# First DFT of the filters: from 64-row tiles with a zero-padded table to tiles of 32 rows and 64 columns

## The chip, the cores and the metric

The kernel runs on one core of a Trainium2 chip. The metric is the time of one execution in microseconds on the device. Five engines work side by side, each with its own list of instructions: TensorE (PE in the profile; its weight loads are listed apart as PEld), VectorE (DVE), ScalarE (ACT), GpSimd (POOL) and SyncE (SP, which here issues most of the DMA transfers). They wait for each other through semaphores.

## The reference

The block takes a sequence of 2048 positions and 512 channels through two parts, each behind a layer norm modulated by six vectors from a conditioning vector. The first part is a long convolution: for each channel a filter K of 2048 taps is built from complex exponentials, and the input is convolved with it by FFTs of length 4096. The second mixes neighbouring positions and channels with four weight matrices.

```python
P = jnp.exp(logdA[:, :, None] * l[None, None, :])
K = jnp.einsum("dn,dnl,dn->dl", Cc, P, dB).real
...
Kf = rfft2(Kp); Uf = rfft2(up)          # K and u padded to twice their length
y = irfft2(Uf * Kf)[..., :L]
y = y.transpose(0, 2, 1) + u * Dskip
...
x = x + ga * A(h)                       # the convolution
x = x + gb * B(h)                       # the MLP part
```

## The kernel before

All stages run from one program whose order is written out by hand (`tc.manual_schedule()`): each engine executes its instructions in the order of the Python calls, and the waits follow from the tiles that they read and write.

1. Filters. `turns`, `exps`, `products` and `burst` (L498) build the filters of all channels and leave them in the SBUF tile KX, 128 partitions by 8192 floats: 64 groups g of 128 floats. Beside that, the input is normalized and goes through its own first DFT (`u_dft`, L426); the result is written to the DRAM tensor VU.
2. `k_first` (L619 to L634), the stage that is changed: the filters' first DFT. The four blocks of 32 partitions of KX each hold 32 points of a different part of the filters, and each needs the same DFT of 32 points by 64 outputs. The groups' floats are the weights (the stationary side); the table FK is the moving side. Eight rounds r of eight groups; each round fills four PSUM banks: one from the pool tile pk1, one from pz, and two named pk2 (through `kbank`). pk1 and pz have two buffers each, pk2 has four, so two rounds fit. ScalarE copies two of the banks into VK[0], VectorE the other two into VK[1] (L632).
3. Sixteen steps over (jh, kc). `spectrum_u` (L650) does the input's second DFT for one block of VU, in two banks named pk1; ScalarE copies them to `us`. `spectrum_k` (L680) does the filters' second DFT from VK[jh] and the twiddle table T2, in two banks pk2. `multiply` (L690, L692) takes the products on VectorE, `back` (L702) transforms on TensorE, ScalarE copies into `z` (two buffers), and GpSimd stores z to the DRAM tensors ZT (L706). SyncE loads the blocks of VU in advance (`load_vu`, L640, seven buffers) and also x (L724), whose tile X2 is the memory of KX.
4. `inverse` (L731) loads ZT back (L721), does the last DFT and adds to x; then comes the second part with its weight matrices (lines L803 to L962), which fills the rest of the time, from some 310 us on.

The order around the change is fixed by the calls: `load_vu` of step 0, `flip(0)` on GpSimd, a small table, the eight rounds of `k_first` with the loads of the next two blocks between them, `spectrum_u` of step 0, and then for each step `spectrum_k`, `multiply`, `back` of the step before and `spectrum_u` of the step after.

Before, FK has two rows of 32 in each half of the partitions and two halves of 64 columns, with zeros where row block and column half do not belong together: one matmul over 64 partitions thus does two blocks, and its 128 columns hold the two results side by side. A bank holds four groups of one 64-row half.

Of the kernel before, what the change touches and what calls it, by code (L numbers as in the profile page):

```python
# [7 lines left out]
F32 = mybir.dt.float32  # L8
# [19 lines left out]
def shape_constants():  # L28
    f = lambda x: np.ascontiguousarray(x.astype(np.float32))
    k1, k2, q = np.arange(32), np.arange(64), np.arange(32)  # L30
    c2b = lambda c: np.where(c < 32, 31 - c, c)
    th = 2 * np.pi * (k1[None] + .5) * q[:, None] / 64
    W = np.stack([np.cos(th), -np.sin(th)], 1)
    Wt = W.transpose(0, 2, 1)
    FU = np.stack([np.stack([Wt, -Wt[..., ::-1]], 1), np.stack([Wt, Wt[..., ::-1]], 1)])
    FU = np.stack([FU, FU])
    FK = np.zeros((2, 2, 32, 2, 64))
    FK[:, 0, :, 0] = FK[:, 1, :, 1] = W.reshape(32, 64)
    b = c2b(np.arange(64))
    al = 2 * np.pi * b[:, None, None] * ((k1[None, :, None] + .5) / 4096 + k2[None, None, :] / 64)  # L40
    c, s = np.cos(al), np.sin(al)
    T2 = np.stack([np.stack([c, -s], 2), np.stack([s, c], 2)]).reshape(128, 32 * 128)
    be = np.arange(32) + .5
    al = 2 * np.pi * be[:, None, None] * ((k1[None, :, None] + .5) / 4096 + k2[None, None, :] / 64)
    TU = np.stack([np.cos(al), np.sin(al), np.cos(al), -np.sin(al)]).reshape(128, 32 * 64)
    al = 2 * np.pi * be[None, :] * k2[:, None] / 64
    cs = np.stack([np.cos(al), np.sin(al)], 2).reshape(64, 64)
    Gm = np.tile(np.concatenate([cs, cs], 1), (2, 1))
    sg = np.array([1.0, -1.0])[:, None]
    th = 2 * np.pi * (k1[:, None, None, None] + .5) * (sg * be[:, None, None] + 64 * q) / 4096  # L50
    FI = np.stack([np.cos(th), -sg * np.sin(th), -np.sin(th), -sg * np.cos(th)]) * (2 / 4096)
    eye = np.eye(16)
    j = np.arange(32)
    c0 = np.tile((eye[:, :, None] * (j + .5)).reshape(16, 512), (2, 1))
    C0 = np.zeros((2, 2, 32, 2, 512))
    C0[:, 0, :, 0], C0[:, 1, :, 1] = c0, c0
    C0 = C0.reshape(128, 1024)
    e1 = (eye[:, :, None] * j).reshape(16, 512)
    e2 = (eye[:, :, None] * np.ones(32)).reshape(16, 512)
    C1 = np.concatenate([e1, e1, e2, e2] * 2, 0)  # L60
    ex0 = np.concatenate([np.arange(31, -1, -1), np.arange(32, 64)])
    ex1 = np.concatenate([64 * np.arange(8), 512 * np.arange(4)])
    CE = np.concatenate([(eye[:, :, None] * ex0.reshape(2, 32)[:, None, None, :]).transpose(1, 0, 2, 3).reshape(16, -1),
                         np.zeros((16, 64 * NX1))], 1)
    CE = np.tile(CE, (8, 1))
    for u in range(4):
        CE[u * 32:u * 32 + 32, 1024 + u * 16 * NX1:1024 + (u + 1) * 16 * NX1] = \
            np.tile((eye[:, :, None] * ex1).reshape(16, -1), (2, 1))
    PA = np.zeros((2, 4, 16, 2, 2, 4, 2, 16))
    PB = np.zeros((4, 2, 16, 4, 4, 2, 4, 16))  # L70
    for e in range(16):
        for v in range(2):
            for u in range(4):
                for p in range(2):
                    PA[v, u, e, v, p, u, p, e] = 1
        for c in range(8):
            for p in range(4):
                PB[c // 2, c % 2, e, c // 4 * 2 + c % 2, p, 1 - c // 2 % 2, p, e] = 1
    return {k: f(v) for k, v in dict(
        FU=FU.reshape(128, 128), FK=FK.reshape(128, 128), T2=T2, TU=TU, G=Gm,  # L80
        FI=FI.reshape(128, 32 * 64), C0=C0, C1=C1, CE=CE, PA=PA.reshape(128, 512), PB=PB.reshape(128, 2048), ID=np.eye(128)).items()}


# [23 lines left out]
def body(ctx, tc, A):  # L107
    nc = tc.nc
    V, S, P, T, Y = nc.vector, nc.scalar, nc.gpsimd, nc.tensor, nc.sync
# [4 lines left out]
    def act(out, in_, f=AF.Copy, scale=1.0, bias=0.0):  # L114
        return S.activation(out, in_, f, bias=bias, scale=scale)  # L115
# [54 lines left out]
    pa12 = a12.enter_context(pool("a12"))  # L170
# [2 lines left out]
    X2 = KX.rearrange("p (b d) -> p b d", b=16)  # L173
    up = a12.enter_context(pool("up", bufs=2))
    wml = a12.enter_context(pool("wml"))
    FK = pa12.tile([128, 128], F32, name="FK")
    sp1 = pa12.tile([128, 1], F32, name="sp1")
    V.memset(sp1, 0.0)
    for i in range(4):
# [4 lines left out]
    ph = a1.enter_context(pool("ph"))  # L184
    FU = ph.tile([128, 2, 64], F32, name="FU")
    DS = ph.tile([128, 128], F32, name="DS")
# [93 lines left out]
    with tc.manual_schedule():  # L280
# [6 lines left out]
        for k, t in (("PA", PA.rearrange("p a b c -> p (a b c)")), ("CE", CE), ("C0", C0),  # L287
                     ("PB", PB.rearrange("p a b c -> p (a b c)")), ("C1", C1)):
            P.dma_start(t, A[k])
        Y.dma_start(FU, A["FU"].rearrange("p (a b) -> p a b", a=2))  # L290
        P.memset(cst, MAGIC)
# [7 lines left out]
        P.tensor_copy(ON.rearrange("p a b -> p (a b)"), cst[:, :384])  # L299
        Y.dma_start(FK, A["FK"])  # L300
        V.tensor_scalar(ld[:, 4:], cT, -1.0, None, op0=OP.mult)
# [118 lines left out]
    def u_dft(b, eo):  # L420
        x = ut[b // 4]
        ps = [psu.tile([128, 512], F32, name="pu") for h in range(2)]
        for i in range(2):
            for h in range(2):
                j = slice(64 * h, 64 * h + 64)
                T.matmul(ps[h][i * 64:i * 64 + 64], FU[j, eo], x[j, b % 4 + i],  # L426
                         start=True, stop=True, skip_group_check=True)
# [79 lines left out]
    for k in range(8):  # L507
        w, i = ("w3", k) if k < 4 else ("w4", k - 4)
        n = A[w].shape[0] // 4
# [18 lines left out]
    T2, TU = [], []  # L528
# [18 lines left out]
    with tc.manual_schedule():  # L547
# [49 lines left out]
        for f in later:  # L597
# [8 lines left out]
    TU = TU[0]  # L606
    Gm = c2.tile([128, 2, 64], F32, name="Gm")
    FI = c2.tile([128, 32, 2, 32], F32, name="FI")
    VK = [v0x.enter_context(pool("v0", side="right")).tile([128, 64, 2, 64], F32, name="VK0"),
          c2.tile([128, 64, 2, 64], F32, name="VK1")]  # L610
# [3 lines left out]
    psa = s2x.enter_context(pool("psa", bufs=2, space=PSUM))  # L614
    psb = s2x.enter_context(pool("psb", bufs=4, space=PSUM))
    kbank = lambda shape: psb.tile(shape, F32, name="pk2")
    block = lambda: ldp.tile([128, 4, 256], F32, name="ld")

    def k_first(r):  # L619
        bank = lambda n: psa.tile([128, 4, 2, 64], F32, name=n)  # L620
        ps = [bank("pk1"), kbank([128, 4, 2, 64]), bank("pz"), kbank([128, 4, 2, 64])]
        kv = KX.rearrange("p (g x) -> p g x", g=64)
        for gl in range(8):
            for j in range(2):
                rows = slice(64 * j, 64 * j + 64)
                T.matmul(ps[2 * j + gl // 4][:, gl % 4].rearrange("p j x -> p (j x)"), kv[rows, r * 8 + gl], FK[rows],  # L626
                         start=True, stop=True)
        for q in (0, 2, 1, 3):
            g0 = r * 8 + q % 2 * 4
            o, i = VK[q // 2][:, :, :, g0:g0 + 4], ps[q].rearrange("p g j x -> p x j g")  # L630
            if q // 2:
                V.tensor_copy(o, i)  # L632
            else:
                act(o, i)  # L634
# [29 lines left out]
    def spectrum_k(jh, kc):  # L664
        p = [kbank([128, 2, 2, 128]) for gh in range(2)]
        for i in range(2):
            for ro in range(2):
                for ri in range(2):
                    for kk in range(2):
                        for gh in range(2):  # L670
                            k1 = kc * 4 + 2 * kk + i
                            rows = slice(gh * 64, gh * 64 + 64)
                            w = T2[k1 // 16][rows, k1 % 16]
                            if ri == gh:
                                w = w[:, ro * 64:ro * 64 + 64]
                            elif ro == ri:
                                w = w[:, gh * 64:gh * 64 + 64]
                            else:
                                w = t3s[kc // 2 * 2][rows, k1 % 8]
                            T.matmul(p[gh][kk * 64:kk * 64 + 64, i, ro], w,  # L680
                                     VK[jh][rows, ri * 32 + k1].rearrange("p j g -> p (j g)"),
                                     start=(ri == 0), stop=(ri == 1), skip_group_check=True)
        return p
# [114 lines left out]
    def transposed(x):  # L798
        ps = [psT.tile([128, 2, 256], F32, name=f"pT{j}") for j in range(2)]
        for j in range(2):  # L800
            for i in range(2):
                for k in range(2 * j, 2 * j + 2):
                    T.transpose(ps[j][:, k % 2, i * 128:i * 128 + 128], x[:, i, k * 128:k * 128 + 128], ident)  # L803
        return ps
# [292 lines left out]
    with tc.manual_schedule():  # L1097
# [3 lines left out]
        for r in range(8):  # L1101
            k_first(r)
            if r == 3:
                load_vu(*steps[1])
            if r == 6:
                load_vu(*steps[2])
        us = spectrum_u(*steps[0])
        split = None
        for n, st in enumerate(steps):
            p = spectrum_k(*st)  # L1110
# [145 lines left out]
        n = cm.tile([128, 2, 512], F32, name="h2")  # L1256
# [18 lines left out]
        r = transposed(n)  # L1275
        split_w(1)
        r = parts_of(r)
# [4 lines left out]
        for g in range(8):  # L1282
            r = chan(g, r)
# [18 lines left out]
```

## Time and profile before

| | |
|---|---|
| runs | 687.0, 689.6, 690.3 us; median 689.6 us |
| the profiled execution | 691.26 us, of which its span (first to last instruction) 689.5 us |
| TensorE | busy 642.6 us, 93% of the span |
| VectorE | busy 498.0 us, 72% |
| ScalarE | busy 331.2 us, 48% |
| GpSimd | busy 124.8 us, 18% |
| granted TensorE clock, mean | 0.989 |
| DMA moved | 86.42 MB, mean 125 GB/s |
| `k_first` on TensorE | from 209.3 to 224.5 us |

How to read the rows that follow. In the profile, L626 is line 626 of the kernel. A row of a group names line, engine and operation, the tiles as out<-in with buffer numbers left out (pk stands for pk1 and pk2), the tile of the array as rows\*columns, the shape, and how many. A float32 matmul appears as two records, each a weight load and a matmul. In the timeline the first number is the start in us from the start of the span, the second the length; brackets give the idle time before and what ended it. In the chain that ended last, each row is a piece of the path, with start, length and place. The rows of the DMA queues give packets, MB and the share of 16 engines' time.

### The profile page before, as it was taken

How to read it: one execution, taken by the hardware profiler on the slowest of the kernel's cores; microseconds unless marked ns; L12 is line 12 of the kernel's file. 1: busy time of each engine (PE TensorE's matmuls, PEld its weight loads, DVE VectorE, ACT ScalarE, POOL GpSimd, SP SyncE). 2: the span in 40 equal slices, each digit the busy share in tenths (PEclk: the TensorE clock that was granted, in tenths of full speed). 3: DMA queues.
4: the chain of work that ended last, by engine and by line, in shares of the span. 5: the costliest groups of instructions: out<-in, count | busy, mean ns of one | idle time of the engine just before them, and what ended most of it. 6: DMA issues, size and time to landing. Idle time of an engine off the chain costs nothing.

```text
span 689.5 us, 16884 instructions
## 1 busy us (share of the span) xinstructions
PE 642.6 (93%) x7195; PEld 509.2 (74%) x7195; DVE 498.0 (72%) x795; ACT 331.2 (48%) x505; POOL 124.8 (18%) x236
## 2 busy tenths in 40 slices
PE   1899999999999998977998999999999999999996
PEld 0456655655569776634887889999899889898895
DVE  7899999999996887986987967464574536363522
ACT  3878988889875557432444623123131312222121
POOL 4011112112103355413741101001010000000000
PEclk9999999999999999998999999999999999999999
DMA  8603264643739997967387010020100201010001
GB/s 299 284 2 79 75 218 105 209 121 85 275 85 317 354 335 258 346 204 226 108 257 240 1 32 32 16 77 15 47 31 17 77 1 62 1 49 13 1 31 31
DMA packets 51091, 86.42 MB, mean 125 GB/s; under 512 B 4676, under 2 KB 39496, under 8 KB 48424
## 3 DMA queue, kind: packets, MB, share of 16 engines
q1 hardware_dynamic: 46712, 66.74, 30.1%
q0 software_dynamic: 3440, 17.57, 7.4%
q8 instruction: 56, 0.92, 0.6%
q10 hardware_dynamic: 864, 1.05, 0.5%
q14 instruction: 19, 0.16, 0.1%
HBM read 59.12 MB, written 32.90 MB: 133 GB/s over the span
## 4 chain that ended last, share of the span: by engine, by line
PE 70%; DVE 6%; DMA 5%; ACT 3%; POOL 2%; issue 1%; ACTq 0%; SPq 0%; DVEq 0%; POOLq 0%
PE pm L841 7%; PE pm L838 7%; PE pm L839 7%; PE xx L448 7%; PE pa L954 6%; PE pa L955 6%; PE pa L962 6%; PE kp L498 3%; DMA ZT<-z 3%; PE ph L893 2%; PE ph L895 2%; PE ph L892 2%; DMA ld<-ZT 2%; PE pu L426 2%; PE pT L803 2%; PE pk L626 2%
## 5 line engine op out<-in xcount | busy, mean ns | idle before, releaser
L115 ACT ACTIVATE gh<-pm 128x512 fp32r<-128x512 f32 (+1 forms) x48 | 26.9, 560 | 200.7 <-PE pm L841 200.7
L838 PE MATMUL pm<-nh,w3h 128*128 128x256 f32 (+1 forms) x352 | 86.6, 281 | 2.7 <-ACT nh L115 2.7
L839 PE MATMUL pm<-nh,w3l 128*128 128x256 f32 (+1 forms) x352 | 86.3, 280 | 0.1
L946 DVE TENSOR_TENSOR gl<-gf,gh 128x512 fp32r<-128x512 f32 (+1 forms) x48 | 30.8, 643 | 68.4 <-ACT gf L115 68.4
L954 PE MATMUL pa<-w4h,gh 128*128 128x512 f32 (+1 forms) x176 | 69.6, 395 | 0.0
L838 PEld LDWEIGHTS pm<-nh,w3h 128*128 128x128 f32 (+1 forms) x352 | 66.0, 187 | 4.4 <-ACT nh L115 2.9
L955 PE MATMUL pa<-w4l,gh 128*128 128x512 f32 (+1 forms) x176 | 68.9, 392 | 0.0
L839 PEld LDWEIGHTS pm<-nh,w3l 128*128 128x128 f32 (+1 forms) x352 | 65.9, 187 | 2.2 <-DVE w3l L756 0.5
L765 POOL TENSOR_TENSOR rs<-mv,eps_t 128x1 f32<-128x1 f32 (+1 forms) x39 | 11.0, 282 | 282.4 <-DVE mv L771 265.4
L841 PE MATMUL pm<-nl,w3h 128*128 128x256 f32 (+1 forms) x352 | 55.0, 278 | 0.0
L449 PE MATMUL xx<-MG,ON 64*128 64x512 f32 x160 | 48.1, 397 | 0.0
L962 PE MATMUL pa<-w4h,gl 128*128 128x512 f32 (+1 forms) x176 | 48.0, 390 | 0.0
L448 PE MATMUL xx<-MG,ON 64*128 64x512 f32 x160 | 48.0, 396 | 0.0
L841 PEld LDWEIGHTS pm<-nl,w3h 128*128 128x128 f32 (+1 forms) x352 | 47.0, 187 | 0.0
L898 DVE TENSOR_TENSOR h<-h,ph 128x512 f32<-128x512 f32 x16 | 11.0, 687 | 45.1 <-PE ph L895 45.1
L466 DVE SCALAR_TENSOR_TENSOR e<-tr,p 128x512 f32<-128x512 f32 x64 | 41.1, 684 | 1.5 <-ACT tr L115 1.5
L498 PEld LDWEIGHTS kp<-e,e 128*32 128x32 f32 x2048 | 30.1, 110 | 12.7 <-issue 7.6
L475 DVE TENSOR_TENSOR e<-tr,p 128x1024 f32<-128x1024 f32 x32 | 39.0, 1220 | 0.0
L476 DVE TENSOR_TENSOR e<-tr,m 128x1024 f32<-128x1024 f32 x32 | 39.0, 1219 | 0.0
L115 ACT ACTIVATE p<-xx 128x1024 f32<-128x1024 f32 (+1 forms) x40 | 37.5, 979 | 2.2 <-PE xx L252 1.0
L962 PEld LDWEIGHTS pa<-w4h,gl 128*128 128x128 f32 (+1 forms) x176 | 33.0, 188 | 7.3 <-DVE gl L946 0.2
L115 ACT ACTIVATE tr<-xx 128x1024 f32<-128x1024 f32 x32 | 33.0, 1030 | 9.6 <-PE xx L449 7.9
(236 smaller groups left out, 1731.6 us busy)
## 6 DMA issues: line engine op xcount, KB each, us to landing
VU<-vs SPq DMA_DIRECT2D x64, 128.0 KB, 3.7
ld<-VU SPq DMA_DIRECT2D x16, 512.0 KB, 7.4
ZT<-z POOLq DMA_DIRECT2D x30, 256.0 KB, 6.2
ld<-ZT SPq DMA_DIRECT2D x12, 512.0 KB
Dw<-in_w POOLq DMA_DIRECT2D x8, 688.0 KB, 4.7
xu<-in_u SPq DMA_DIRECT2D x4, 1024.0 KB, 8.0
KX<-in_x SPq DMA_DIRECT2D x4, 1024.0 KB, 8.0
GD<-go SPq DMA_DIRECT2D x16, 256.0 KB, 2.3
```

The costliest lines, as they stand in the source:

```text
L115: return S.activation(out, in_, f, bias=bias, scale=scale)
L448: T.matmul(x[:, :512], la, ma, start=(i == 0), stop=(i == len(ops) - 1))
L449: T.matmul(x[:, 512:], lb, mb, start=(i == 0), stop=(i == len(ops) - 1))
L466: V.scalar_tensor_tensor(e0[:, 1, a], tr[:, 1, 0], 1.0 - 2.0 * a, mg[:, a], op0=OP.mult, op1=OP.mult)
L475: V.tensor_mul(e0[:, 0], tr[:, 0, 0:1].to_broadcast([128, 2, 512]), mg)
L498: T.matmul(kp[32 * j:32 * j + 32, (k % 2) * 4 + g], e1[:, r, d], e0[:, r, :, d * 32:d * 32 + 32], start=(r == 0), stop=(r == 1), skip_grou ...
L838: T.matmul(p, wh[:, k, c], hi[k], start=(k == 0), stop=False)
L839: T.matmul(p, wl[:, k, c], hi[k], start=False, stop=False)
L841: T.matmul(p, wh[:, k, c], lo[k], start=False, stop=(k == 3))
L954: T.matmul(acc[i], gh[:m, e, s], W4h[:m, f], start=(f == 0), stop=False)
L955: T.matmul(acc[i], gh[:m, e, s], W4l[:m, f], start=False, stop=False)
L962: T.matmul(acc[i], gl[:m, e, s], W4h[:m, f], start=False, stop=(f == 10))
```

## The change

The table is now the plain 32 by 64 table, four times below each other (128 partitions by 64 columns, no zeros). Each matmul takes 32 partitions (row tile q) and 64 of the group's 128 floats (column half c), so that a group takes eight matmuls instead of two, each with half the moving columns. Row tile q writes to the bank `ps[q]`, which now holds all eight groups of the round for that row tile. The copies out take one bank each, as before, into the part of VK that belongs to q; the order of the copies, the engines and the buffers are the same. The result in VK is the same.

```diff
-    FK = np.zeros((2, 2, 32, 2, 64))
-    FK[:, 0, :, 0] = FK[:, 1, :, 1] = W.reshape(32, 64)
+    FK = np.tile(W.reshape(32, 64), (4, 1))
...
-    FK = pa12.tile([128, 128], F32, name="FK")
+    FK = pa12.tile([128, 64], F32, name="FK")
...
     def k_first(r):
-        bank = lambda n: psa.tile([128, 4, 2, 64], F32, name=n)
-        ps = [bank("pk1"), kbank([128, 4, 2, 64]), bank("pz"), kbank([128, 4, 2, 64])]
+        bank = lambda n: psa.tile([128, 8, 64], F32, name=n)
+        ps = [bank("pk1"), kbank([128, 8, 64]), bank("pz"), kbank([128, 8, 64])]
         kv = KX.rearrange("p (g x) -> p g x", g=64)
         for gl in range(8):
-            for j in range(2):
-                rows = slice(64 * j, 64 * j + 64)
-                T.matmul(ps[2 * j + gl // 4][:, gl % 4].rearrange("p j x -> p (j x)"), kv[rows, r * 8 + gl], FK[rows],
-                         start=True, stop=True)
+            for c in range(0, 128, 64):
+                for q in range(4):
+                    rows = slice(32 * q, 32 * q + 32)
+                    T.matmul(ps[q][c:c + 64, gl], kv[rows, r * 8 + gl, c:c + 64], FK[rows],
+                             start=True, stop=True, skip_group_check=True)
         for q in (0, 2, 1, 3):
-            g0 = r * 8 + q % 2 * 4
-            o, i = VK[q // 2][:, :, :, g0:g0 + 4], ps[q].rearrange("p g j x -> p x j g")
+            o, i = VK[q // 2][:, :, q % 2, r * 8:r * 8 + 8], ps[q].rearrange("p g x -> p x g")
             if q // 2:
                 V.tensor_copy(o, i)
             else:
                 act(o, i)
```

More of the change, by code (lines that the diff above doesn't have):

```diff
@@ L79, in shape_constants @@
     return {k: f(v) for k, v in dict(
-        FU=FU.reshape(128, 128), FK=FK.reshape(128, 128), T2=T2, TU=TU, G=Gm,
+        FU=FU.reshape(128, 128), FK=FK, T2=T2, TU=TU, G=Gm,
         FI=FI.reshape(128, 32 * 64), C0=C0, C1=C1, CE=CE, PA=PA.reshape(128, 512), PB=PB.reshape(128, 2048), ID=np.eye(128)).items()}
```

## The prediction

> **What bounds the kernel now.** I read the page first, then a table of the stretches around the changed stage, then the chain that ended last, then the timeline engine by engine, then the DMA of the stretches that follow.
>
> ```profile
> span 689.5 us, 16884 instructions
> PE 642.6 (93%) x7195; PEld 509.2 (74%) x7195; DVE 498.0 (72%) x795; ACT 331.2 (48%) x505; POOL 124.8 (18%) x236
> 209.27:212.84 3.57, 3.57 (x64) 3.57 (x64) 1.93 (x3) 0.05 (x1) 3.37 (x3) 1.00 1.02 398
> 213.44:224.50 11.06, 11.06 (x196) 10.94 (x200) 8.04 (x12) 7.92 (x15) 1.99 (x2) 1.00 0.94 301
> ```
>
> The last two lines are two stretches of the changed stage: length, then busy time of PE, PEld, DVE, ACT and POOL, granted clock, DMA share, GB/s. PE is busy for all of both; DVE and ACT, which copy out, for some 72%. So inside the stage TensorE sets the pace. The whole stage is about 15 of 689.5 us, which caps everything below.
>
> ```profile
> 207.39 5.42 DMA xu<-in_T
> 212.81 0.59 ACT VK L115
> 213.44 0.37 PE pk L626
> ...
> 224.43 1.02 PE pk L650 x16
> 225.45 1.82 PE pk L680 x64
> ...
> 227.31 0.69 DVE ma L690
> ...
> 234.17 8.87 DMA ZT<-z
> ...
> 243.20 0.60 ACT z L115
> ```
>
> This is the chain: start, length, what. k_first starts on PE at 209.27 but ScalarE cannot write VK before a transfer lands at 212.81; PE, out of banks, stands from 212.84 to 213.44. From there L626 carries the chain, then the first spectra (L650, L680), the first multiply at 227.31, and soon a store that takes 8.87 us to land while ScalarE's next copy into z waits for it. The stage is on the path, but only for what lies after 213.44.
>
> **The change: the matmuls.** Before, 8 rounds r of 16 matmuls; each fp32 matmul is two records, 256 in all (192 + 64).
>
> ```profile
> L626 PE MATMUL pk<-FK,KX x192: 272/272/373, 209.3 to 224.2; 64*128 64x128 f32 x192
> L626 PE MATMUL pz<-FK,KX x64: 272/272/373, 209.3 to 223.3; 64*128 64x128 f32 x64
> 209.48 0.27 PE L626 MATMUL pk<-FK,KX 64*128 64x128 f32 x1
> 209.49 0.27 PE L626 MATMUL pz<-FK,KX 64*128 64x128 f32 x1
> 209.59 0.27 PE L626 MATMUL pk<-FK,KX 64*128 64x128 f32 x1
> 206.99 1.10 PE L498 MATMUL kp<-e,e 128*32 128x64 f32 x64
> 225.49 0.27 PE L680 MATMUL pk<-VK,T 64*64 64x128 f32 x1
> 225.50 0.27 PE L680 MATMUL pk<-VK,xu 64*64 64x128 f32 x1
> 225.51 0.27 PE L680 MATMUL pk<-VK,T 64*64 64x128 f32 x1
> 225.51 0.27 PE L680 MATMUL pk<-VK,xu 64*64 64x128 f32 x1
> ```
>
> Two row tiles start 0.01 apart and come again after 0.11 us: a tile takes its next 128-column record every 0.11. So a round is 16 turns x 0.11 = 1.8 us. After the change a round has 8 x 2 x 4 = 64 matmuls, 128 records, on eight tiles (four row, two column) of 64 weight columns and 64 moving columns. For 64 moving columns the row is L498: 64 records in 1.10 us, the last 0.22 long, so (1.10 - 0.22)/63 = 14.0 ns each over four tiles, 56 ns per turn. Between different tiles four starts lie within 0.02 us (225.49 to 225.51), about 7 ns apart. Eight tiles x 7 = 56 ns: issue just keeps up with the tiles. A round is then 16 x 57 = 0.91 us, against 1.8.
>
> No row shows eight tiles, so the ends are: 14.0 ns per record (no denser than L498) gives 1.79 us a round, as now; 7 ns gives 0.91. I take 0.91, since 14.0 is what four tiles leave idle, not what issue needs.
>
> **The change: the copies out.** Each round still fills four banks of 512 columns, and ScalarE and VectorE still copy two each.
>
> ```profile
> 212.79 2.56 ACT L115 ACTIVATE VK<-pk 128x512 f32<-128x512 f32 x5 [4.04 <-DMA xu<-in_T]
> 215.53 0.60 ACT L115 ACTIVATE VK<-pk 128x512 f32<-128x512 f32 x1 [0.18 <-PE pk L626]
> 211.40 0.69 DVE L632 COPY VK<-pk 128x512 f32<-128x512 f32 x1 [0.20 <-PE pk L626]
> 212.29 0.69 DVE L632 COPY VK<-pz 128x512 f32<-128x512 f32 x1 [0.20 <-PE pz L626]
> 229.11 0.68 DVE L690 TENSOR_TENSOR mb<-pk,us 128x512 f32<-128x512 f32 x1
> 229.71 0.68 DVE L692 TENSOR_TENSOR zc<-ma 128x512 f32<-128x512 f32 x1
> 224.04 0.39 PE L626 MATMUL pk<-FK,KX 64*128 64x128 f32 x4
> 224.36 1.09 PE L650 MATMUL pk<-ld,wm 64*64 64x256 f32 x16
> ```
>
> Now VectorE copies every 0.89 us (211.40, 212.29), waiting 0.20 each time. Back to back it takes a 128x512 tile every 0.60 (229.11, 229.71), ScalarE every 0.49 (five in 2.56). The new runs of eight floats instead of four in the copies I cost at nothing: these paces come from copies and products of the same size with other patterns.
>
> What is new is when a bank is ready. Before, half the banks were full after four of a round's eight groups; now every bank gets its last record at the end of the round, so both copies of an engine start together, later. And with two sets of banks, round r+2 needs all four copies of round r. Per two rounds: matmuls 0.91, 0.29 from the last record's start to a copy's start, copies 0.60 + 0.69 to the end of VectorE's second, 0.04 to PE (212.81 + 0.59 to 213.44): 2.53 us, 1.27 a round. Below TensorE's 1.8, above 0.91: the copies and the banks become the bound.
>
> The sum, in order. Rounds 0 and 1 run until about 211.1, then wait for ScalarE, which starts at 212.79 whatever PE does. Round 2 now needs both of its copies of round 0 (0.49 + 0.60 after 212.79 = 213.88), so it starts at 213.92, not 213.44: 0.48 lost. Round 3 follows at 214.90, and by the 2.53-cycle round 7 starts at 220.2 and its last record at 221.1. L650 then needs two pk1 banks, and the second is round 7's, copied at 221.4 to 222.0 (before, that bank had been copied half a round earlier): L650 truly starts at 222.0 against 224.36. That is 0.6 us of new wait, in the sum. ScalarE's last VK copy ends at 222.5, before L680 needs it at 222.9; the first multiply comes at 225.0 against 227.31: **2.3 us earlier**. The table FK is half as long and is loaded 200 us before use: nothing.
>
> **What survives behind it.**
>
> ```profile
> DMA packets 1550, 3.36 MB, mean 373 GB/s; under 512 B 77, under 2 KB 1293, under 8 KB 1293
> DMA packets 608, 0.75 MB, mean 251 GB/s; under 512 B 27, under 2 KB 587, under 8 KB 587
> SPq L640 <- PE pk L650: 9.9, 3, 4.3
> ACT z L115 <- DMA ZT<-z: 8.7, 3, 4.3
> ```
>
> The first line is the DMA of 225 to 234, the second that of 232 to 235. The queues are full from the loads of blocks and of x until 232, so issuing earlier does not land earlier there; the slack is the dip, 3 us x (373 - 251)/373 = 1.0 us. The third line (SP's waits from 209 to 234) says that block loads are released by L650, so these do move with PE. So at the store that ends at 243 between 1.0 and 2.3 us survive; I take 1.5, nearer the full queue. Farther on DVE and PE work densely and nothing returns what is won, but the z copies wait for stores (8.7 us from 225 to 310, fourth line), where either end is possible.
>
> The profiled execution took 691.26 us, 1.76 more than its span; 691.26 - 1.5 = 689.8. It stands 1.7 above the median of 689.6, so against that median the forecast is **688.1 us**. A change of 0.5% is 3.4 us, about what can be told from none; the runs before spread from 687.0 to 690.3.
>
> **The rivals.**
>
> *Absorbed.* The stage ends 2.3 us sooner and the full queue gives none of it on: the store still lands near 243. For it: 373 GB/s throughout; against it: the dip. 689.6.
>
> *Carried and amplified.* All 2.3 us arrive, and the stores, issued earlier beside the same loads, halve one of the z waits (4.3 at most, so 2.2): 685.1. Against it: more transfers in flight tend to lengthen such waits.
>
> *Instruction supply.* PE has to be fed four times as many instructions.
>
> ```profile
> q8 instruction: 56, 0.92, 0.6%
> q8 instruction: 3, 0.05, 1.2%
> GD<-go SPq DMA_DIRECT2D x16, 256.0 KB, 2.3
> ```
> The instruction queue brought 0.92 MB in 56 packets: 16.4 KB each, and over 2 x 7195 records 64 B an instruction, so 256 instructions a packet. From 209 to 225 it brought three (second line). A new round is exactly 256 instructions, eight packets for the stage. A packet takes 0.6% x 16 x 689.5/56 = 1.2 us of its engine, below the 1.27 of a round: hidden. If they come one at a time with the whole 2.3 us that the quickest transfer on the page needs from issue to landing, round 7 starts at 213.92 + 5 x 2.3 = 225.4, its last record at 226.3, L650 at 227.2: 2.9 us later than now, 692.5. Above 2.4 us a packet it is slower by over 0.5%. For it: PE never took instructions at such a pace. Against: packets are asked for ahead.
>
> *Slower: the eight tiles do not issue densely.* If records keep L680's pace, 1.82 us for 64, 28 ns, a round is 3.6 us, round 7 ends near 235.8, L650 starts 12.3 us late: 701.9. It decides from 16.9 ns a record: (224.36 + 3.4 - 0.93 - 213.92)/6 = 2.15 us a round, over 128. For it: no row has eight tiles; against: the 7 ns steps between tiles.
> The Trainium skill, "TensorE: Matmul & The Clock Gate", section "Wait — 56ns, not 53.3ns?", says that matmul starts never come closer than about 25 ns however small they are. By that rule a round would be an estimated 3.2 us and the time an estimated 699.3; this trace already disagrees wherever tiles differ (7 ns steps, 14.0 ns on average for L498), so I read the floor as one tile's and leave it little.
>
> **How the numbers follow.** Forecast (1.0 to 2.3 us gained) 0.44; absorbed 0.18; carried and amplified past 0.5% 0.15; instruction supply or L498's pace, zero to 3.4 us lost, 0.14; slower by more 0.09 (0.05 for sparse issue, 0.04 for packets over 2.4 us). Faster by over 0.5% 0.15; within 0.5% 0.44 + 0.18 + 0.14 = 0.76; slower 0.09. The range 685.3 to 692.5 leaves out the slower case and the far end of the amplified one; the forecast's own is 687.3 to 688.6, and the runs' spread lies on top.
>
> **What would show it.** Right: L626 with 1024 records of 32x64, eight starts within some 0.055 us; rounds every 1.27 us from 213.9, PE waiting at L626 for VK's copies by DVE and ACT; DVE copies in pairs 0.60 apart; first L690 near 225.0; the store near 241.5 instead of 243. Wrong: records over 14 ns apart on average, PE idle at L626 put down to issue (supply), ScalarE starting later than 212.8, or the first multiply early and the store's landing unmoved.

## The result, and the profile after

The changed kernel takes 711.55 us (median; 710.9 to 713.5) against 689.43 us before: a ratio of 1.033, 95% interval 1.030 to 1.037. The forecast was 688.1 us. Its profiled execution has a span of 711.8 us, 22.3 longer than that of before (689.5).

The page of the changed kernel: span, the table of engines, the granted clock over the span, the instruction queue, the chain's shares.

```profile
span 711.8 us, 18420 instructions
PE 648.0 (91%) x7963; PEld 512.4 (72%) x7963; DVE 497.6 (70%) x795; ACT 330.5 (46%) x505; POOL 124.8 (18%) x236
PEclk9999999999995599998999999999999999999999
q8 instruction: 62, 1.02, 0.6%
PE 61%; DVE 23%; DMA 5%; issue 5%; ACT 3%; POOL 2%; SPq 0%; ACTq 0%; DVEq 0%; POOLq 0%
```

The 768 additional records and six additional packets of instructions are there as counted. New are two slices with the clock at half, and "issue", time in which an engine waited for nothing that the profile shows: 5% of the chain's span against 1% before. The waits of TensorE from 205 to 255 us, and its weight loads in the timeline wherever a wait stands ahead of them, name the place:

```profile
PEld pk L626 <- issue: 19.6, 8, 4.6
...
211.56 0.17 PEld L626 LDWEIGHTS pk<-FK,KX 32*64 32x64 f32 x1 [2.78 <-issue]
215.57 0.18 PEld L626 LDWEIGHTS pk<-FK,KX 32*64 32x64 f32 x1 [1.86 <-issue]
222.04 0.18 PEld L626 LDWEIGHTS pk<-FK,KX 32*64 32x64 f32 x1 [4.33 <-issue]
228.78 0.18 PEld L626 LDWEIGHTS pk<-FK,KX 32*64 32x64 f32 x1 [4.60 <-issue]
232.24 0.18 PEld L626 LDWEIGHTS pk<-FK,KX 32*64 32x64 f32 x1 [1.31 <-issue]
235.69 0.18 PEld L626 LDWEIGHTS pk<-FK,KX 32*64 32x64 f32 x1 [1.31 <-issue]
239.42 0.17 PEld L626 LDWEIGHTS pk<-FK,KX 32*64 32x64 f32 x1 [1.59 <-issue]
243.42 0.18 PEld L626 LDWEIGHTS pk<-FK,KX 32*64 32x64 f32 x1 [1.85 <-issue]
```

TensorE stops eight times within the stage and starts again eight times, with no engine or transfer to wait for that the profile names. How much it does between two stops is in the table by stretches (length, then PE, PEld, DVE, ACT, POOL busy with their counts, clock, DMA share, GB/s) and in the instruction queue's row for the stretch from 228.7 to 232.2:

```profile
215.50:222.00 6.50, 2.33 (x128) 2.15 (x128) 1.29 (x2) 1.08 (x2) 0.00 (x0) 0.50 0.95 313
222.00:228.70 6.70, 2.34 (x128) 2.15 (x128) 1.29 (x2) 1.09 (x2) 0.00 (x0) 0.50 0.93 327
228.70:232.20 3.50, 2.33 (x128) 2.14 (x128) 1.29 (x2) 1.09 (x2) 0.00 (x0) 0.50 0.05 19
232.20:235.60 3.40, 2.33 (x128) 2.14 (x128) 1.29 (x2) 1.08 (x2) 0.00 (x0) 0.50 0.02 5
...
q8 instruction: 1, 0.02, 1.6%
```

Each time exactly 128 matmuls and 128 weight loads, 256 instructions: one packet. TensorE runs a packet in some 2 us, then stands until the next has come. One packet comes in each of these stretches. While the DMA queues are full (313 and 327 GB/s) a packet's turn takes 6.5 and 6.7 us; when they are empty (19 GB/s and less) it still takes 3.45 to 4.0 (from 228.78 on). The stage runs from 207.99 to 244.69, 36.7 us instead of 15.2, and the first multiply comes at 249.63 instead of 227.31: 22.3 us late, all of the loss. On its way in, the stage shows what the eight tiles can do with instructions at hand:

```profile
208.11 0.22 PE L626 MATMUL pz<-FK,KX 32*64 32x64 f32 x1
208.12 0.23 PE L626 MATMUL pk<-FK,KX 32*64 32x64 f32 x3
...
208.17 0.22 PE L626 MATMUL pz<-FK,KX 32*64 32x64 f32 x1
208.18 0.23 PE L626 MATMUL pk<-FK,KX 32*64 32x64 f32 x3
...
208.23 0.22 PE L626 MATMUL pz<-FK,KX 32*64 32x64 f32 x1
```

The rows shown are every second group of four starts. The same tile's records (pz) come again after 0.06 us with seven others between them: eight starts in 58 to 59 ns, close to the 57 of the prediction. That lasts for three turns or so; then the starts spread, for a reason that stays open, and at 208.71 the buffered instructions are used up. Only 67 matmuls and 67 weight loads, about half a round, were at hand when the stage began.

### The profile page after: what moved, and what is told of

The parts are those of the page before. It is cut to its first block, busy times and chain, and to the rows that moved or that the text cites. A ratio compares the mean times of both kernels' runs of the same rounds, so it can differ in the third digit from the quotient of the medians.

```text
span 711.8 us, 18420 instructions
## 1 busy us (share of the span) xinstructions
PE 648.0 (91%) x7963; PEld 512.4 (72%) x7963; DVE 497.6 (70%) x795; ACT 330.5 (46%) x505; POOL 124.8 (18%) x236
## 4 chain that ended last, share of the span: by engine, by line
PE 61%; DVE 23%; DMA 5%; issue 5%; ACT 3%; POOL 2%; SPq 0%; ACTq 0%; DVEq 0%; POOLq 0%
PE pm L840 7%; PE pm L837 7%; PE pm L838 7%; PE pa L953 6%; PE pa L954 6%; PE pa L961 6%; DVE e L465 4%; DVE e L475 4%; DVE e L474 4%; PE pk L679 2%; PE pk L626 2%; DVE m L471 2%; PE pz L701 2%; PE xx L447 2%; PE pk L649 2%
## 5 line engine op out<-in xcount | busy, mean ns | idle before, releaser
L448 PE MATMUL xx<-MG,ON 64*128 64x512 f32 x160 | 47.1, 390 | 0.0
L447 PE MATMUL xx<-MG,ON 64*128 64x512 f32 x160 | 47.1, 389 | 0.0
L679 PE MATMUL pk<-VK,xu 64*64 64x128 f32 x768 | 38.7, 274 | 0.0
```

Source lines behind the costliest of these rows:

```text
L447: T.matmul(x[:, :512], la, ma, start=(i == 0), stop=(i == len(ops) - 1))
L679: T.matmul(p[gh][kk * 64:kk * 64 + 64, i, ro], w, VK[jh][rows, ri * 32 + k1].rearrange("p j g -> p (j g)"), start=(ri == 0), stop=(ri == 1 ...
```

## Experiments

Theory S: TensorE's instructions come in packets of 256, one on its way at a time, and the stage now asks for more than that brings. Rival T: the eight small tiles, or four row tiles, are slow. Rival C: the halved clock is the cause. The ratios are to the kernel before, run beside each experiment. A stage's length is from its first matmul to the end of its last.

**The same number of instructions without the small row tiles.** Before's table, 64-row tiles, banks and copies; each matmul cut into four.

```diff
-                T.matmul(ps[2 * j + gl // 4][:, gl % 4].rearrange(...), kv[rows, r * 8 + gl], FK[rows], ...)
+                for c in range(0, 128, 64):
+                    for h in range(2):
+                        T.matmul(ps[2 * j + gl // 4][c:c + 64, gl % 4, h], kv[rows, r * 8 + gl, c:c + 64],
+                                 FK[rows, 64 * h:64 * h + 64], ...)
```

> k_first as before (table with zero blocks, 64-row tiles, banks and copies of before), but each matmul cut into four of 64 weight columns and 64 moving columns: 64 matmuls a round, as many PE instructions (256 a round, 2048 in all) as the changed kernel, in four 64x64 tiles instead of eight 32x64. Theory S (PE's instructions come in packets of 256 and only one is asked for at a time, so a round of 256 waits for its packet): the L626 stage lasts 34 to 38 us like the changed kernel's 36.6, with PE's waits put down to issue, and the time is 708 to 714 us. Rival T (the eight small tiles or the four row tiles are what is slow): four tiles at L498's 14.0 ns a record make 1.8 us a round as before, 688 to 692 us.

Measured: 710.7 us, ratio 1.031 (1.027 to 1.034); the stage lasts 36.2 us. The waits of PE's matmuls in the stretch from 205 to 260, of this kernel and of the changed one:

```profile
PE pk L628 <- issue: 15.5, 8, 5.1
...
PE pk L626 <- issue: 18.2, 8, 4.4
```

T falls: with half as many, larger tiles and the zero blocks still in, the same count of instructions costs the same time.

**32 rows by 128 columns, half the instructions.**

```diff
-            for c in range(0, 128, 64):
-                for q in range(4):
-                    T.matmul(ps[q][c:c + 64, gl], kv[rows, r * 8 + gl, c:c + 64], FK[rows], ...)
+            for q in range(4):
+                T.matmul(ps[q][:, gl], kv[rows, r * 8 + gl], FK[rows], ...)
```

> The changed kernel with row tiles of 32 but all 128 weight columns: 32 matmuls a round instead of 64, so 128 PE instructions a round (1024 in all), four row tiles, the same four banks and copies. Theory S: half as many packets; four of them beyond what is buffered, at 3.5 to 6.5 us each: L626 stage 18 to 22 us, time 692 to 698 us. Rival T (row tiles of 32): no better than the changed kernel, above 704 us. What the prediction said (copies and banks set the pace, no starvation): 687 to 690 us.

Measured: 700.6 us, ratio 1.015 (1.011 to 1.020), the stage 26.7 us: over what S expected, below T's. And the reason is another one. Its stretch from 219 to 225 us, and its weight loads:

```profile
219.00:225.00 6.00, 6.00 (x120) 6.00 (x120) 1.75 (x4) 1.84 (x4) 0.00 (x0) 0.50 1.11 360
...
L625 PEld LDWEIGHTS pk<-FK,KX x384: 181/328/334, 208.1 to 234.3; 32*128 32x128 f32 x192
```

PE is busy all of it, with a turn of the four tiles every 0.21 us at a clock of 0.50. At full clock, at the start of the stage, a turn took 0.112 us, as with 128 moving columns before, so halving the moving columns alone wins nothing. That the load of 128 weight columns sets the turn fits this, since tiles with 64 of each came again after 0.06 us. At half clock the turn nearly doubles. This kernel is hardly starved (0.5 us of waits put down to issue): the halved clock paces it. How much of the loss is the clock's alone is not shown, for a kernel below with as many instructions and about a quarter of the TensorE work loses nearly as much.

**The queues kept quiet.** The changed kernel with the loads behind a small transfer that needs the last round's copy.

```diff
             k_first(r)
-            if r == 3:
-                load_vu(*steps[1])
-            if r == 6:
-                load_vu(*steps[2])
+        Y.dma_start(HOLD, VK[1][0:1, 0, 0, 56:64])
+        load_vu(*steps[1])
+        load_vu(*steps[2])
```

> The changed kernel with the block loads after the first, and the loads of x, held back until the last round has been copied out, so that the DMA queues are quiet during most of k_first. Theory S: the long waits of 4 us (a packet standing behind data) fall to the short ones; every round takes about 3.45 us, L626 stage 26 to 30 us instead of 36.6; the whole is not much better, 700 to 714 us, because the loads come late. Rival C (the halved clock is what makes the rounds long): the stage stays at 35 to 38 us.

Measured, one execution: 707.1 us, stage 29.6 us, waits for issue 11.8 instead of 18.2 us:

```profile
PE pk L627 <- issue: 11.8, 8, 2.3
```

As S expected: the waits of 4 us are gone (longest 2.3), the short ones stay although from 219 on nothing else moves. The restarts are 3.45 to 4.0 us apart. So a packet has a way of about 3.5 to 4 us of its own, and full queues add up to 3 us.

**A busy TensorE.** The changed kernel with two long matmuls ahead of each round.

```diff
+        for q in range(2):
+            T.matmul(ps[q].rearrange("p g x -> p (g x)"), kv[:, r * 8], KX[:, r * 1024:r * 1024 + 512], ...)
```

> The changed kernel with two float32 matmuls of 128x128 by 512 columns ahead of each round (their result is overwritten): 8 more instructions a round, but some 1.7 us more of TensorE work, so that the clock is not let down by idleness. Theory S: the stage stays as long, 34 to 40 us, and the time 708 to 716 us, whatever the clock. Rival C (clock): at a granted clock of 1.0 the rounds need 0.9 us for the small matmuls and 1.7 for the long ones, so the stage is 20 to 23 us and the time 694 to 700 us.

Measured, one execution: 714.1 us, stage 34.1 us. Its stretch from 231 to 237, the same stretch of the kernel with 64x64 tiles, and the first and last row of the first round:

```profile
231.00:237.00 6.00, 6.00 (x263) 4.18 (x263) 2.08 (x4) 1.96 (x4) 0.00 (x0) 1.00 0.02 5
231.00:237.00 6.00, 4.40 (x271) 4.13 (x266) 2.44 (x4) 2.26 (x4) 0.00 (x0) 1.00 0.02 5
...
211.22 0.27 PE L629 MATMUL pk<-FK,KX 32*64 32x64 f32 x2
...
212.59 0.22 PE L629 MATMUL pk<-FK,KX 32*64 32x64 f32 x1
```

The clock is full but for 3.4 us from 223.5 on, and the kernel is no faster. From 225.7 to 243.2 a packet comes every 3.5 us, as at half clock. The kernel with 64x64 tiles, also at full clock in this stretch, is starved there too (busy 4.40 of 6.00 us). So C is not what makes the changed kernel slow.

The last two rows show something else. Here a whole round of eight tiles ran without a stop, and its 128 records start within 1.37 us, some 11 ns apart, not within the 0.91 us of the prediction.

**Some of the rounds.** Even rounds in the new form; then the last round alone (the same source, with `r == 7`).

```diff
+    def k_first(r):
+        (k_tiles if r % 2 == 0 else k_zero)(r)
```

> Rounds 0, 2, 4 and 6 as in the changed kernel (32x64 tiles, 256 PE instructions), rounds 1, 3, 5 and 7 as before (64), all from the table of before: 1280 instructions in the stage. Theory S (one packet of 256 instructions on its way at a time, 3.5 to 6.5 us each): five packets after what is buffered, the last some 21 to 24 us after the first record, so the stage ends 6 to 9 us late and the time is 695 to 699 us, between the two kernels by its instructions. Rival T (something in the eight small tiles): half of the changed kernel's loss, 700 to 702 us.

> Only round 7 as in the changed kernel, the other seven as before: 704 PE instructions in the stage instead of 512. Theory S: the packet under way covers the 192 more, no starvation; round 7 takes 0.9 us instead of 1.8 and its copies are ready 0.6 us later, so 688 to 691 us, no difference. This shows the eight tiles at their own pace. Rival T: 2 to 3 us of the changed kernel's loss, 692 us.

Measured: even rounds 702.2 us, ratio 1.020 (1.018 to 1.022); last round 693.6 us, ratio 1.007 (1.006 to 1.009). Both are slower than S's figures. For the even rounds it is over half of the loss, T's number, though the first run had ruled T out. The trace shows what S's figure left out: in the full queue the packets started 6.2 and 7.2 us apart (213.24, 220.47, 226.68), and the clock was at 0.50 from 224.8 to 235.0, which stretches the last rounds. For the last round the weight loads show what the expectation missed:

```profile
225.81 0.13 PEld L645 LDWEIGHTS pk<-FK,KX 32*64 32x64 f32 x1 [2.15 <-issue]
```

192 instructions more, and the last round stands 2.15 us for a packet. The kernel before was already close to what the packets bring here: in its trace, too, one started at 223.2, just ahead of the end of the stage, but without a stop. The profiled execution is the quickest of six (691.3 us), and its first multiply is 2.6 us late; where the rest of the 4.0 us between the medians goes is not shown.

**Less TensorE work with no more instructions.** Before's tiles, banks and copies, both operands cut to their upper 16 bits (the filters' spectrum gets coarse): one record a matmul.

```diff
+        kb = KX.bitcast(mybir.dt.bfloat16).rearrange("p (g x two) -> p g x two", g=64, two=2)
+        FB = FK.bitcast(mybir.dt.bfloat16).rearrange("p (x two) -> p x two", two=2)
...
-                ... kv[rows, r * 8 + gl], FK[rows],
+                ... kb[rows, r * 8 + gl, :, 1], FB[rows, :, 1],
```

> The kernel before with k_first's matmuls on the upper 16 bits of both operands (bfloat16, so the filters' spectrum is coarse): same tiles, banks and copies, but one record a matmul instead of two, 32 PE instructions a round instead of 64. TensorE's work in the stage is halved or better with no more instructions: what the change meant to do. Prediction's steps: copies set the pace at about 1.2 us a round, the first multiply comes 2 to 3.4 us earlier (224 to 225.3), of which 1 to 2.3 us arrive: 687 to 688.7 us. Rival A (the full DMA queue absorbs it): first multiply as early, time 689 to 690.5 us.

Measured: 686.85 us, ratio 0.997 (0.995 to 0.999). From its timeline: ScalarE's sixteen copies in one piece, two of VectorE's, and the first multiply.

```profile
212.06 8.57 ACT L115 ACTIVATE VK<-pk 128x512 f32<-128x512 f32 x16 [4.72 <-DMA xu<-in_T]
214.37 0.68 DVE L633 COPY VK<-pz 128x512 f32<-128x512 f32 x1
214.97 0.68 DVE L633 COPY VK<-pk 128x512 f32<-128x512 f32 x1
...
224.94 0.69 DVE L691 TENSOR_TENSOR ma<-pk,us 128x512 f32<-128x512 f32 x1 [4.12 <-PE pk L681]
```

The copies set the pace (0.54 us each on ScalarE, 0.60 on VectorE) and the first multiply comes 2.4 us earlier. Not all of this is the change: in this execution the transfer that ScalarE waits for landed 0.7 us sooner than before (212.06 instead of 212.79), while the halved clock (0.58 from 219 to 225) held the first spectra back. By the ratio 2.1 us arrive (0.3% of 689.6; 1.0 to 3.2 by the interval); the time is just under the 687 that was expected. Rival A, that the queue absorbs it, expected a ratio of 1 and lies outside the interval, if barely.

**The changed kernel with that arithmetic.** 32x64 tiles, half its instructions, a quarter of the 32x128 kernel's TensorE work.

```diff
-                    T.matmul(ps[q][c:c + 64, gl], kv[rows, r * 8 + gl, c:c + 64], FK[rows], ...)
+                    T.matmul(ps[q][c:c + 64, gl], kb[rows, r * 8 + gl, c:c + 64, 1], FB[rows, :, 1], ...)
```

> The changed kernel (32x64 tiles, its banks and copies) with the upper 16 bits of both operands (bfloat16, so the filters' spectrum is coarse): one record a matmul, 128 PE instructions a round, as many as the 32x128 kernel, but a quarter of its TensorE work. Theory S: 1024 instructions need three to four packets after what is buffered, the last at 222 to 229 us; first multiply at 228 to 232 us, 691 to 696 us, although TensorE has next to nothing to do. Rival W (the 32x128 kernel was late by its weight loads at half clock alone): copies set the pace as in the bfloat16 kernel in 64-row tiles, 686 to 688.5 us.

Measured: 697.6 us, ratio 1.012 (1.009 to 1.015). Two of its weight-load rows and a stretch:

```profile
223.31 1.55 PEld L627 LDWEIGHTS <-KX 32*64 32x64 bf16 x126 [4.71 <-issue]
...
229.78 0.63 PEld L627 LDWEIGHTS <-KX 32*64 32x64 bf16 x60 [4.43 <-issue]
219.00:225.00 6.00, 1.63 (x126) 1.41 (x126) 1.74 (x4) 1.32 (x3) 0.00 (x0) 0.50 1.09 349
```

TensorE is busy 1.63 of 6 us and the stage still lasts 21.9, for its packets. Against the 16-bit kernel above, with the same arithmetic and a quarter of the instructions, it is 10.8 us slower. W falls for this kernel, and S's mechanism is seen; its price was again too low, by 1.6 us.

**The 16-bit kernel with its clock held.** Two 16-bit matmuls of 512 columns ahead of each round of the kernel that gained.

```diff
+        for q in range(2):
+            T.matmul(ps[q].rearrange("p g j x -> p g (j x)"), kb[:, r * 8, :, 1], kb[:, r * 8:r * 8 + 4, :, 1], ...)
```

> The bfloat16 kernel in 64-row tiles with two bfloat16 matmuls of 128x128 by 512 columns ahead of each round (overwritten): 4 instructions and some 0.45 us of TensorE work a round. In the profile of that kernel the clock was at 0.5 from 213.8 to 224.1 us, which stretches the first spectra. If busy matmuls hold the clock, the stage keeps its pace (copies), the first spectra run at full clock, the first multiply comes 1 to 1.6 us earlier (223.3 to 224) and the time is 685 to 686.5 us. Rival: the added work delays as much as the clock gives, 686.5 to 688 us.

Measured: 686.6 us, ratio 0.996 (0.994 to 0.998). The stretches from 219 to 225, first without and then with them:

```profile
219.00:225.00 6.00, 5.85 (x102) 4.67 (x101) 1.88 (x5) 3.10 (x6) 0.00 (x0) 0.58 1.12 364
219.00:225.00 6.00, 6.00 (x131) 4.16 (x130) 3.88 (x7) 4.75 (x9) 0.00 (x0) 1.00 1.09 358
```

The clock is held from 217.8 on, the first multiply is at 224.76 instead of 224.94: the added work takes what the clock gives, as the rival had it. Both 16-bit kernels in 64-row tiles beat the kernel before by 0.3 to 0.4%, at the price of a coarser spectrum. In full float32 nothing here beats the kernel before.

## Why the prediction was wrong

The step that failed is the instruction supply. The prediction had it as a rival, from the right rows: a round is exactly one packet of 256, and PE never took instructions at such a pace. It went wrong in the price, and gave packets over 2.4 us a chance of 0.04. I took 1.2 us from the packet's time on its engine, "hidden" below a round of 1.27, and at most 2.3 us, the quickest transfer on the page. Measured, from one packet's start on TensorE to the next: 3.45 to 4.0 us with empty queues, 6.5 to 6.7 with full ones, on average 4.55 over seven packets (211.56 to 243.42, the last start). The page of before could have told: its block loads and stores took a median of 6 to 8 us to land, and the quickest transfer was the wrong end for a bound from above. The price alone does not make up the whole: at 4.55 us the rival's formula, five packets after 213.92, gives a round 7 at 236.7. Measured by counting records, round 7 starts at 240.3, where the forecast had 220.2. The rest is the start: rounds 0 and 1 were to run freely until 211.1, but the instructions at hand ended after half a round, at 208.71. That a packet is asked for ahead helped only before the stage: in it, one is under way at a time.

The Trainium skill, "Runtime: NRT & Kernel Launch", section "Instruction fetch mechanics", says that instructions are refilled in blocks of 256 while the engine executes, and that the cost is mostly hidden. The trace agrees on the 256; with a block used up in about 2 us it was not hidden, by up to 4.6 us a block.

The other steps, as far as the runs reach:
- Eight tiles with a turn of 57 ns: seen for three turns (208.11 to 208.23). For a whole round the term was too small: with instructions at hand it took 1.37 us instead of 0.91. In the prediction's cycle, two rounds then take 2.99 us instead of 2.53, and by an estimate from these numbers some 1.5 of the 2.3 us gained would have been lost even with instructions always at hand.
- Copies and banks as the next bound, first multiply 2.3 us earlier at 225.0: the 16-bit kernel, in the old tiles, is paced by its copies and has the multiply at 224.94. That the number fits so well is in part luck, by the transfer that landed sooner. In the changed kernel VectorE and ScalarE waited for PE in every round.
- 1.0 to 2.3 us surviving: 2.1 us in the 16-bit kernel, with an interval (1.0 to 3.2) that cannot tell the ends apart. The losses passed on almost whole as well: 22.3 of 22.3 us in the changed kernel, 18.4 of 19.7 in the one with 64x64 tiles (spans against first multiplies).
- The slower rival by sparse issue of the eight tiles was wrong in its place: the 28 ns a record it feared is what the packets allow, 3.45 us for 128, whatever the tiles.
- Not considered: that the clock falls to half in the stage (0.50 from 210.7 us on in the changed kernel). It cost the changed kernel little, since it waited for packets anyway, as the run with the long matmuls shows; it paced the 32x128 kernel, at a cost that the runs do not separate from that of its packets.

## What to carry to other kernels

Cutting matmuls into small tiles multiplies TensorE's instructions: before doing so, count them by the stretch, not by the kernel, and compare with what the instruction queue brought in the densest stretch of the trace. Here about 256 instructions per 3.45 us were the most that a stage got once its buffer was empty, and about half of that beside full DMA queues. Bound a transfer that has never been on the path by what transfers take in that stretch, not by the quickest on the page. A stage can be tested for it by changing the number of instructions at the same work, or the work at the same number.

## What the runs showed that was not expected

A wait for instructions carries no name: the profile puts it down to "issue", and stops after every 256 instructions are its sign.

The clock stayed at 0.50 for 27 us in the 32x128 kernel (from 211.2) although PE was busy in its records throughout (6.00 of 6.00 us in the stretch shown). The Trainium skill, "TensorE: Matmul & The Clock Gate", section "What's actually happening", ties the halved clock to idleness; by the records there was none in that time. Long matmuls ahead of the rounds kept the clock at 1.00 in two kernels, but for 3.4 us in each. What the chip counts as activity there stays open.
